# Transposing q of batch 1 with the DMA crossbar instead of TensorE, and the output of half batch 1 in two parts

## Chip, cores and metric

One core of a Trainium2 chip. The time is device microseconds (us) of one execution; a kernel's time is the median of its runs. A run counts as slow when it is over 1.5% above the fastest of its kernel; that happened in gated (one run of four) and early (three of four) alone. "Before" was run beside every other kernel on the same chip; a ratio is the mean time of one kernel's fast runs over that of the other's of the same rounds, with a 95% interval, so it is not quite the ratio of the medians quoted next to it.

## The reference, cut to what matters

Block attention (4 batches, 8 heads, 768 tokens, head size 64), in which keys and values are first mixed by a matrix P that a Sinkhorn iteration makes from `sort_net`; then a feed-forward layer (512 to 2048 to 512) with a squared ReLU.

```python
k_sorted = einsum('bhij,bhjcd->bhicd', P, k_b)      # 8 blocks of 96 tokens
v_sorted = einsum('bhij,bhjcd->bhicd', P, v_b)
attn = softmax(scale * q_b @ k_sb^T)                # within a block
x = (attn @ v_sb)                                   # -> 3072 tokens x 512
out = (s * relu(x @ w_in)**2 + b) @ w_out
```

## The kernel before

TensorE is given the FFN of one half batch while the attention of the next is mixed in between, from a queue of small pieces. Q has to be transposed (`QT`, head size on the partitions). For batches 2 and 3 the DMA crossbar does it (`q_turn`), for batches 0 and 1 TensorE does:

```python
def q_piece(b, hp0, eng):                 # two of the four head pairs
    ...
    for i in range(2):
        for t in range(TQ):               # TQ = 6 groups of 128 tokens
            for e in range(2):
                nc.tensor.transpose(out=ps[e*64:(e+1)*64, i, t*128:(t+1)*128],
                                    in_=qr[b][:, 2*(hp0+i)+e, t, :], identity=ident)
    evac(QT[b][:, hp0:hp0+2, :]..., ps[:, :, 0:S]..., eng)

def q_turn(b):
    for t in range(TQ):
        nc.sync.dma_start(out=QT[b][:, :, t*128:(t+1)*128],
                          in_=qr[b][:, t].rearrange("p h d -> p (h d)"), transpose=True)
```

Mixed V of batch 1 goes through DRAM, because the next step wants another layout: `v_piece1` writes it in 12 pieces ("dv"), `v_read` reads it back in two halves ("vs", 6144 runs of 128 bytes). Both use the sync engine's queue, which issues in program order.

```python
    V1(4)(); V1(5)()                       # last dv writes
    q_piece(1, 0, "s")
    ...
    csums(0, 8)                            # GpSimd: sums of w_out
    v_read(1, nc.sync)
    ffn1(1, ...)                           # FFN of half batch 1, first layer
    load_v(*brows(3))
    csums(8, NF)                           # GpSimd, until about 64.6 us
    qu = Queue([nothing, seq(lambda: q_piece(1, 2, "s"), K(1, 0, 16, "v")), nothing,
                seq(K(1, 32, 16, "s"), K(1, 64, 16, "v")), nothing,
                seq(lambda: load_k(*brows(2)), lambda: load_q(2), bias_piece),
                V2[0], S2(2, 0), V2[1], S2(2, 2), V2[2], V2[3], P2(2, 0), ...], 24)
    ffn2(0, qu)                            # P2(2, 0) is the first product with vs
```

`load_k` of batch 2 (64 rows of 12 KB) and `load_q` of batch 2 (6144 runs of 128 bytes) stand in that queue.

The softmax here doesn't subtract the row's maximum and nothing guards it: scores larger than these inputs give would overflow.

## Time and profile before

| | before |
|---|---|
| time, median of 3 runs | 231.67 us (231.25 to 231.69) |
| span of the profiled run | 229.8 us |
| TensorE busy | 223.2 us, 97% |
| first product with vs starts | 75.62 us |

In the profile's lines PE is TensorE, PEld its loading of weights, DVE VectorE, ACT ScalarE, POOL GpSimd and SPq the sync engine's queue; L342 is line 342 of the kernel. The timeline of the sync queue (start, length, issuing queue, line, what):

```profile
38.59 16.51 SPq L342 DMA_DIRECT2D dv<-vn  x12
62.30 2.27 SPq L361 DMA_DIRECT2D vs<-dv  x2
```

then that of GpSimd:

```profile
64.59 0.54 POOL L97 DMA_DIRECT2D kb<-in_k_dram  x1
65.13 5.29 POOL L84 DMA_DIRECT2D qr<-in_q_dram  x6
```

The vs read is asked for at 62.30, k of batch 2 at 64.59, q of batch 2 from 65.13 on. The read has a head start of 2.3 us.

### The profile page before, as it was taken

How to read it: one execution, taken by the hardware profiler on the slowest of the kernel's cores; microseconds unless marked ns; L12 is line 12 of the kernel's file. 1: busy time of each engine (PE TensorE's matmuls, PEld its weight loads, DVE VectorE, ACT ScalarE, POOL GpSimd, SP SyncE). 2: the span in 40 equal slices, each digit the busy share in tenths (PEclk: the TensorE clock that was granted, in tenths of full speed). 3: DMA queues.
4: the chain of work that ended last, by engine and by line, in shares of the span. 5: the costliest groups of instructions: out<-in, count | busy, mean ns of one | idle time of the engine just before them, and what ended most of it. 6: DMA issues, size and time to landing. Idle time of an engine off the chain costs nothing.

```text
span 229.8 us, 4833 instructions
## 1 busy us (share of the span) xinstructions
PE 223.2 (97%) x2034; PEld 136.3 (59%) x2034; DVE 116.0 (50%) x244; ACT 115.7 (50%) x165; POOL 48.1 (21%) x62
## 2 busy tenths in 40 slices
PE   8979999999999999999999999999999999999994
PEld 5879888765554565665555555655555556654442
DVE  4778666638991554344345843434443634441221
ACT  5268479685358387866621285565322245660000
POOL 7920000299992000008730000000000000000000
PEclk9995699999999999999999999999999999999999
DMA  5899999999399998645999996610115250001212
GB/s 93 137 199 214 223 195 205 227 219 203 70 122 180 314 247 136 126 116 70 133 142 150 183 176 134 76 47 0 49 46 121 87 114 0 3 0 46 86 54 91
DMA packets 46694, 28.90 MB, mean 126 GB/s; under 512 B 35920, under 2 KB 41040, under 8 KB 46160
## 3 DMA queue, kind: packets, MB, share of 16 engines
q0 software_dynamic: 18800, 15.21, 46.5%
q1 hardware_dynamic: 27728, 13.32, 26.8%
q8 instruction: 16, 0.26, 0.5%
q10 hardware_dynamic: 144, 0.07, 0.1%
q14 instruction: 6, 0.05, 0.1%
HBM read 29.63 MB, written 8.65 MB: 167 GB/s over the span
## 4 chain that ended last, share of the span: by engine, by line
PE 80%; DMA 14%; ACT 3%; DVE 1%; issue 0%; SPq 0%
PE hps L498 31%; PE ops L552 30%; DMA dv<-vn 8%; DMA vs<-dv 6%; PE wp L182 6%; PE pv L402 4%; PE sc L375 3%; PE tv L320 2%; PE ops L537 2%; PE tk L294 1%; ACT ks L240 1%; PE tq L254 1%; ACT qt L240 1%; PE tv L350 0%; ACT rt L513 0%
## 5 line engine op out<-in xcount | busy, mean ns | idle before, releaser
L498 PE MATMUL hps<-xt,wi 128*128 128x384 bf16 (+1 forms) x576 | 87.0, 308 | 0.2
L552 PE MATMUL ops<-wo,gt 128*128 128x512 bf16 x368 | 85.8, 379 | 0.0
L498 PEld LDWEIGHTS <-wi 128*128 128x128 bf16 x576 | 53.7, 98 | 30.6 <-issue 1.1
L513 ACT ACTIVATE rt<-hps 128x768 bf16<-128x768 f32 (+1 forms) x72 | 53.1, 740 | 37.0 <-PE hps L498 36.1
L514 DVE TENSOR_TENSOR gt<-rt 128x768 bf16<-128x768 bf16 (+1 forms) x72 | 41.6, 580 | 49.5 <-ACT rt L513 49.3
L552 PEld LDWEIGHTS <-gt 128*128 128x128 bf16 x368 | 34.0, 98 | 37.9 <-issue 0.6
L378 ACT ACTIVATE at<-sc 96x768 bf16<-96x768 f32 x32 | 24.4, 803 | 30.2 <-PE sc L375 30.1
L526 DVE SCALAR_TENSOR_TENSOR ot<-ops,s_bc,bias 128x512 f32<-128x512 f32 x23 | 17.2, 750 | 40.4 <-PE ops L552 40.3
L407 DVE TENSOR_TENSOR x<-pv,rec 96x512 bf16<-96x512 f32 (+1 forms) x36 | 22.6, 628 | 1.3
L240 ACT CAST ks<-tk 64x512 bf16<-64x512 f32 (+1 forms) x32 | 18.6, 582 | 4.2 <-PE tk L294 3.9
L674 POOL TENSOR_TENSOR csum<-csum,wo 128x512 f32<-128x512 f32 x14 | 17.6, 1254 | 1.0
L182 PE MATMUL wp<-zt 128*128 128x256 bf16 x84 | 13.5, 329 | 1.1 <-DVE warm L113 1.1
L402 PEld LDWEIGHTS <-at 96*128 96x128 bf16 (+1 forms) x256 | 12.0, 104 | 4.3 <-DMA vs<-dv 0.8
L238 DVE CAST ks<-tk 64x512 bf16<-64x512 f32 (+1 forms) x20 | 13.1, 654 | 2.1 <-PE tk L294 1.8
L402 PE MATMUL pv<-vs,at 96*128 96x66 bf16 (+1 forms) x256 | 13.0, 199 | 0.4 <-DMA vs<-dv 0.3
L240 ACT CAST vn<-tv 128x512 bf16<-128x512 f32 (+1 forms) x12 | 9.4, 800 | 6.8 <-DMA out_dram<-ot 3.8
L84 POOL DMA_DIRECT2D qr<-in_q_dram x12 | 10.6, 913 | 5.3 <-DMA kb<-in_k_dram 2.9
L375 PEld LDWEIGHTS <-ks 64*96 64x96 bf16 x256 | 8.3, 128 | 5.7 <-issue 4.3
L406 DVE RECIPROCAL rec<-pv 96x8 f32<-96x8 f32 (+1 forms) x36 | 6.9, 193 | 9.1 <-PE pv L402 9.1
L182 PEld LDWEIGHTS <-zt 128*128 128x128 bf16 x84 | 9.5, 117 | 3.2 <-DVE warm L113 1.1
L375 PE MATMUL sc<-qt,ks 64*96 64x96 bf16 x256 | 10.7, 219 | 0.0
L240 ACT COPY qt<-tq 128x768 bf16<-128x768 bf16 (+1 forms) x6 | 5.9, 1014 | 5.0 <-PE tq L254 3.3
(72 smaller groups left out, 97.5 us busy)
## 6 DMA issues: line engine op xcount, KB each, us to landing
out_dram<-ot SPq DMA_DIRECT2D x23, 256.0 KB, 2.8
kb<-in_k_dram POOLq DMA_DIRECT2D x4, 768.0 KB, 11.1
vb<-in_v_dram POOLq DMA_DIRECT2D x4, 768.0 KB, 18.9
wi<-in_moe_w_in_dram POOLq DMA_DIRECT2D x2, 1024.0 KB, 19.6
wo<-in_moe_w_out_dram POOLq DMA_DIRECT2D x2, 1024.0 KB, 32.5
qr<-in_q_dram POOLq DMA_DIRECT2D x12, 128.0 KB, 17.7
dv<-vn SPq DMA_DIRECT2D x6, 256.0 KB, 6.6
vs<-dv POOLq DMA_DIRECT2D x4, 384.0 KB, 13.1
```

Of the source, the lines that this page charges most:

```text
L182: nc.tensor.matmul(out=wp, lhsT=zt[:, 0:128], rhs=zt, start=True, stop=True)
L240: nc.scalar.copy(out=out, in_=in_)
L375: nc.tensor.matmul(out=sc[:, e, n * BLK:(n + 1) * BLK], lhsT=ks[pr, g0 + n, :], rhs=QT[b][pr, hp, q0:q0 + BLK], start=True, stop=True)
L378: nc.scalar.activation(out=at, in_=sc[:, :, 0:TG], func=AF.Exp, scale=scale)
L402: nc.tensor.matmul(out=pv[e][0:m, (n - n0) * VW:(n - n0 + 1) * VW], lhsT=atf[:, c0:c0 + m], rhs=VS[b][:, gi, :], start=True, stop=True)
L407: nc.vector.tensor_tensor(out=x[:, n0:n0 + nn, hp * 128:(hp + 1) * 128].rearrange("p n (e d) -> p e n d", e=2), in0=pvv[:, :, :, 0:D], in1 ...
L498: nc.tensor.matmul(out=hps[:, f, 0:nt], lhsT=wi_at(hp, f0 + f), rhs=xt_at(t, hp, n0, nn), start=(hp == 0), stop=(hp == NHP - 1))
L513: nc.scalar.activation(out=rt[:, :, 0:nt], in_=hps[:, :, 0:nt], func=AF.Relu)
L514: nc.vector.tensor_tensor(out=gt[:, f0:f0 + 2, c0:c0 + nt], in0=rt[:, :, 0:nt], in1=rt[:, :, 0:nt], op=ALU.mult)
L526: nc.vector.scalar_tensor_tensor(out=ot, in0=ops, scalar=s_bc, in1=bias, op0=ALU.mult, op1=ALU.add)
L552: nc.tensor.matmul(out=ops, lhsT=gt[:, f, m * 128:(m + 1) * 128], rhs=wo_at(f), start=(f == 0), stop=(f == NF - 1))
L674: nc.gpsimd.tensor_tensor(out=csum, in0=csum, in1=wo_at(f), op=ALU.add)
```

## The change

The intent: take 48 transposes from TensorE, which works 97% of the time, and let the crossbar do them. The load has to become token-major for that: within a partition the eight heads of one token lie side by side, and the runs shrink from 768 to 128 bytes. Since the first `q_piece` had filled TensorE's wait for the copy of the transposed output, that output is now transposed and copied in two parts.

```diff
     def load_q(b, part=slice(0, 128)):
-        if b > 1:
+        if b > 0:
             qr[b] = qrp.tile([128, TQ, H, D], BF, tag="qr", name=f"qr{b}")
             for t in range(TQ):                    # six loads, 64-element runs
...
-    def q_piece(b, hp0, eng):   (removed)
...
-                   seq(V1(2), V1(3)), lambda: t_piece(1, "v")], 8), 2, 2)
+                   seq(lambda: t_part(1, 0, "s", 0, HB), V1(2), V1(3)),
+                   lambda: t_part(1, 2, "v", 0, HB)], 8), 2, 2)
     V1(4)()
     V1(5)()
-    q_piece(1, 0, "s")
...
     csums(0, 8)
+    q_turn(1)
     v_read(1, nc.sync)
...
-    qu = Queue([nothing, seq(lambda: q_piece(1, 2, "s"), K(1, 0, 16, "v")), nothing,
+    qu = Queue([nothing, K(1, 0, 16, "v"), nothing,
```

## The prediction

> **What bounds the kernel now.** I read the page first (busy shares, then the chain of work that ended last), then the chain in order of time, then the DMA queues stretch by stretch between 34 and 86 us, where everything that the change touches happens. The page:
>
> ```profile
> span 229.8 us, 4833 instructions
> PE 223.2 (97%) x2034; PEld 136.3 (59%) x2034; DVE 116.0 (50%) x244; ACT 115.7 (50%) x165; POOL 48.1 (21%) x62
> ```
>
> TensorE works 97% of the span. Of its 6.6 us without work about 1.1 lie ahead of the first matmul and 3.4 after the last one, so the middle is a nearly unbroken row of matmuls: what shortens TensorE's list shortens the kernel, unless a wait takes its place. The chain in order of time (start, length, what) says where such a wait stands ready:
>
> ```profile
> 42.82 11.82 DMA dv<-vn
> 54.66 7.50 DMA dv<-vn
> ...
> 62.69 12.89 DMA vs<-dv
> 75.62 0.71 PE pv L402 x16
> ```
>
> For 33 us, from 42.8 to 75.6, the chain is not TensorE at all. V of batch 1, mixed by the sort matrix, is written to DRAM in 12 pieces (dv) and read back in another layout (vs), and the first product that needs it starts the moment it lands. The list of TensorE's waits between 37 and 95 us puts the price at only
>
> ```profile
> PE pv L402 <- DMA vs<-dv: 0.3, 1, 0.3
> ```
>
> (total, times, longest). So at 75.6 us two chains meet almost exactly: TensorE's own work, and a DMA round trip with no slack to speak of. The whole change lies ahead of this meeting point.
>
> The tile view of qr gives the transposes that go away (ns min/median/max, starts):
>
> ```profile
> L269 PE MATMUL tq<-ident,qr x48: 218/219/244, 45.8 to 60.1; 128*64 128x128 bf16 x48
> L279 SPq DMA_TRANSPOSE qt<-qr x12: 1197/1216/2528, 91.7 to 147.2; - x12
> ```
>
> and the timeline shows that they don't cost 48 times 219 ns, because they are pipelined:
>
> ```profile
> 45.81 0.86 PE L269 MATMUL tq<-ident,qr 128*64 128x128 bf16 x24
> 59.41 0.86 PE L269 MATMUL tq<-ident,qr 128*64 128x128 bf16 x24
> ```
>
> Last, the load queue of the DMA (q0) in two stretches of 4 us, 34 to 38 and 82 to 86 (packets, MB landed, share of 16 engines):
>
> ```profile
> q0 software_dynamic: 958, 0.81, 127.9%
> ```
>
> ```profile
> q0 software_dynamic: 2708, 0.34, 133.6%
> ```
>
> The first moves runs of 768 and 1024 bytes at about 200 GB/s of bf16. The second is q of batch 2, already loaded token-major, in runs of 64 elements (128 bytes): 677 packets per us, but only 85 GB/s.
>
> **What the Trainium skill says.** "DMA: Bandwidth & Descriptors", section Specifications, gives 512 B as the least transfer for line rate; the two lines above agree in direction (85 against 200 GB/s). The same page, section Queues, rings and completion order, says that each engine takes turns between the queues that have work for it, at packet granularity. The trace agrees: the dv writes issued at 38.6 us, beside short packets, landed in 5.3 us, and those of 43 us, which drained beside the 12 KB rows of k, in 11.8 us. "Advanced Engine Details and Errata", section X-Bar Transpose (TRN2), calls crossbar transposes as fast as regular DMAs. No view isolates one here; what I see is issue on the sync queue, 1.2 us each, 2.5 us to landing. "TensorE: Matmul & The Clock Gate", section Part 4: PE-mode transpose, reports about 275 ns for one in a kernel; 219 ns is recorded here, and 36 ns apart is what 24 of them cost the engine.
>
> **The change, part by part.**
>
> 1. TensorE loses 48 transposes: 2 x 0.86 = 1.72 us. This is the most that the change can take from the engine's list. ScalarE loses two 1.44 us copies of qt, which delayed nothing that TensorE waited for.
>
> 2. The first 0.86 us is a filler. Before, it ran at 45.8 while VectorE copied all of xt for half batch 1 (0.94 us from 45.72), and the FFN started at 46.72, right behind both. Now that copy is split: four transposes' worth of heads on ScalarE (0.80 us for 128x768, as the qt copies of that form take) ahead of two vn copies, the rest on VectorE (0.55 us) after the last gt. I walk it: t_part ends on TensorE at 43.7; ScalarE copies it until 44.6, two vn follow (0.47 apart) until 45.5, the last rt until 46.0; VectorE makes gt until 46.45 and the second xt until 47.0. TensorE, through with V1 at 46.2, does two products on the first half of xt (0.33 us) and waits for the second until 47.0. Work equal to a start at 46.7: the gain of this half is about 0.05 us. The extra copy on ScalarE gives back what the filler cost.
>
> 3. The second 0.86 us (59.4) is real up to the next wait. At 65.17 TensorE multiplies csum, which GpSimd finishes at about 64.75 (14 additions of 1.25 us, last start 63.5). TensorE would now come at 64.3, so about 0.4 us of wait appears and some 0.45 us of gain remains, if the second half of w_out, which the last eight additions read, is there by 54.1 as before (it landed at 12.72 + 36.3 = 49.0).
>
> 4. The load of q grows from 1024 packets of 768 bytes to 6144 of 128. At 200 GB/s the old one is 3.9 us (the trace: from 37.95, w_out's first half, to 41.85). At 677 per us the new one is 9.1 us. Everything behind it in the same queue moves by about 5.3 us: w_out's second half from 49.0 to 54.3, k of batch 1 from 51.8 to 57 (first used about 59.3), the two v loads of batches 2 and 3 from 55.6 and 62.0 to about 61 and 66 (first used about 66.2). Each lands within a microsecond of its need. GpSimd's six issues (0.9 us each instead of one) wait for earlier loads' slots but are ahead of the queue's need.
>
> 5. Six crossbar transposes go onto the sync queue between the last dv write and the vs read: 6 x 1.2 = 7.3 us of issue, plus 0.79 MB of traffic. In the old pace (last dv write issued at 54.7) they would end at 62.4, where the vs read was issued anyway (62.3). If the dv writes come sooner, because they now meet 128-byte packets until 47 instead of 12 KB rows, the transposes start about 48 and the vs read could be issued at 56 to 58.
>
> Sum on TensorE alone: 0.05 + 0.45, and the 0.3 us of the old wait, if vs lands a microsecond earlier: -0.5 to -1.2 us.
>
> **The rivals.**
>
> A. Clean gain: the dv writes land faster, vs is issued before 60, all loads just make it. For it: the DMA was only 30% busy with loads from 58 to 62, so there is air; and small packets overlap with another queue's large ones (in 82 to 86 us q1 moved 0.70 MB beside those 2708). Time 230 to 231.
>
> B. The wait takes its place: the DMA engines carry 5.3 us more of q and an estimated 3 us of transposes before the same deadline, so vs or the last v load comes late. From 47.2: 5.2 for w_out, 3.9 for each of k, v, v, 2 for dv, 3 for transposes, 9.1 for the vs read (6144 packets) make 78 without overlap, against the 74.9 at which TensorE now wants vs; with k of batch 2 in between, up to 82. For it: the same sum for before, 41.85 + 5.2 + 11.7 + 2 + 9.1 + 3.9 = 73.8, is close to the real 75.6. Time 232 to 237.
>
> C. TensorE waits earlier: w_out's second half comes at 55 instead of 54.1, csum slips 1 us, and the product for the bias with it. This eats the gain and leaves 231.5 to 232.5.
>
> D. Nothing: vs lands where it did, and TensorE waits out what it saved: 231.4.
>
> Against a large effect in either direction: the ceiling of 1.72 us, and the fact that after 76 us nothing of the list changes.
>
> **Range and chances.** A gain beyond 2% would need 4.6 us and TensorE gives up 1.7, so its chance is 0.01. A loss beyond 2% needs the full, unoverlapped sum of B: 0.09. I weigh A at 0.45, C and D together at 0.3, B at 0.25, and put the time at 231.1 us, with 229.4 to 235.2 as the range.
>
> **What would show it.** Right for step 1: no line for tq<-ident,qr of form 128*64, TensorE's busy time 221.5. Step 2: a wait of TensorE of about half a microsecond near 46.5 for the xt copy. Step 3: csum as releaser of the bias product. Step 4: w_out's second half landing at 54 to 55, longer loads of k. Step 5: dv writes of 42 to 47 us landing in under 6 us and the vs read issued before 60; if it is issued after 62 or lands after 75, B holds. The prediction is wrong if the token-major load drains much faster or slower than 677 packets per us, if crossbar transposes stall the other traffic while they run, or if the vs wait disappears and more than 1.7 us is won.

## The result, and the profile after

242.45 us (median of 4 runs, 242.25 to 243.07) against 231.46 beside it: ratio 1.0483, interval 1.0455 to 1.0511. The change makes the kernel 4.8% slower. The page of the changed kernel:

```profile
span 240.7 us, 4740 instructions
...
PE 223.3 (93%) x1967; PEld 136.4 (57%) x1986; DVE 118.6 (49%) x244; ACT 113.6 (47%) x164; POOL 52.7 (22%) x67
```

TensorE's busy time has not fallen although it has 48 transposes fewer; we come to that. (Its count has fallen by 67: 19 matmuls of the output layer are missing from this trace.) The chain in order of time:

```profile
60.45 1.33 SPq L265
61.88 1.22 SPq L265
63.19 1.22 SPq L265
64.50 1.22 SPq L265
65.81 0.54 SPq L347
66.40 17.86 DMA vs<-dv
84.39 1.09 PE pv L388 x16
85.49 1.71 PE ops L538 x4
```

L265 are the crossbar transposes. The sync queue works through them and comes to the vs read (L347) at 65.81; the read's second half then needs 17.86 us where it needed 12.89; the product that waits for it starts at 84.39 instead of 75.62. The waits of TensorE (total, times, longest):

```profile
PE pv L388 <- DMA vs<-dv: 8.1, 1, 8.1
PE hps L484 <- DVE xt L238: 1.1, 1, 1.1
```

The timelines of the sync queue, then of GpSimd, answer to those of before:

```profile
39.44 16.79 SPq L328 DMA_DIRECT2D dv<-vn  x11
...
56.33 9.39 SPq L265 DMA_TRANSPOSE qt<-qr  x6
...
65.81 8.61 SPq L347 DMA_DIRECT2D vs<-dv  x2
```

```profile
64.93 0.55 POOL L97 DMA_DIRECT2D kb<-in_k_dram  x1
65.46 5.29 POOL L84 DMA_DIRECT2D qr<-in_q_dram  x6
```

The read is now asked for 0.9 us after k of batch 2, not 2.3 us ahead of it. In the DMA queues between 66 and 70 us (packets, MB, share of 16 engines), before:

```profile
q1 hardware_dynamic: 2436, 0.31, 128.1%
q0 software_dynamic: 21, 0.26, 34.5%
```

and after:

```profile
q0 software_dynamic: 44, 0.54, 92.7%
q1 hardware_dynamic: 328, 0.08, 10.7%
```

Before, q1 (the sync queue) moves 2436 packets of vs in these 4 us. After, it moves 328, none of vs, while q0 moves two thirds of k.

One more loss follows from the wait. This is the stretch after it (window; its length; then busy us and instructions of PE, PEld, DVE, ACT, POOL; granted TensorE clock; DMA share; GB/s):

```profile
84.40:87.00 2.60, 2.60 (x21) 1.48 (x22) 1.69 (x4) 0.00 (x0) 0.00 (x0) 0.50 1.05 405
87.00:90.00 3.00, 3.00 (x19) 1.32 (x18) 0.00 (x0) 1.01 (x1) 0.00 (x0) 0.55 0.23 89
```

TensorE comes back at half its clock. "TensorE: Matmul & The Clock Gate", section Why this matters for your kernels, warns of gaps over about 3 us between bursts; the trace agrees, with 0.50 after a gap of 8.1 us. By these two lines the half clock lasted some 5.3 us after the wait. Slow matmuls count as busy: at half the clock 5.3 us hold about 2.7 us of extra busy time (an estimate), more than the 1.7 us of transposes that went away.

The sum, between landmarks of the two chains. Up to the first product with vs: 84.39 - 75.62 = 8.77 us. From there to the first layer for half batch 2 (102.30 and 90.99 us): 17.91 - 15.37 = 2.54 us, close to the estimate for the clock. From there to the end: 138.40 - 138.81 = -0.41 us. Together 10.9 us, the difference of the spans.

### The profile page after: what moved, and what is told of

Same layout as the page of the kernel before. It is cut to its first block, busy times and chain, and to the rows that moved or that the text cites. A ratio compares the mean times of both kernels' runs of the same rounds, so it can differ in the third digit from the quotient of the medians.

```text
span 240.7 us, 4740 instructions
## 1 busy us (share of the span) xinstructions
PE 223.3 (93%) x1967; PEld 136.4 (57%) x1986; DVE 118.6 (49%) x244; ACT 113.6 (47%) x164; POOL 52.7 (22%) x67
## 4 chain that ended last, share of the span: by engine, by line
PE 73%; DMA 14%; POOL 4%; SPq 3%; ACT 2%; issue 2%; DVE 1%; POOLq 0%
PE hps L484 30%; PE ops L538 29%; DMA vs<-dv 7%; DMA qr<-in_q_dram 4%; PE pv L388 4%; PE sc L361 3%; POOL csum L660 3%; DMA vb<-in_v_dram 3%; SPq L265 2%; PE tv L306 2%; PE ops L523 1%; PE tk L280 1%; ACT ks L240 1%; PE tq L254 1%; PE wp L182 1%
## 5 line engine op out<-in xcount | busy, mean ns | idle before, releaser
L538 PE MATMUL ops<-wo,gt 128*128 128x512 bf16 x349 | 84.7, 385 | 1.6 <-DVE ot L512 0.4
L500 DVE TENSOR_TENSOR gt<-rt 128x768 bf16<-128x768 bf16 (+1 forms) x72 | 44.9, 630 | 48.2 <-ACT rt L499 48.0
L538 PEld LDWEIGHTS <-gt 128*128 128x128 bf16 x368 | 34.5, 99 | 39.1 <-issue 2.6
L388 PE MATMUL pv<-vs,at 96*128 96x66 bf16 (+1 forms) x256 | 13.6, 203 | 8.2 <-DMA vs<-dv 8.1
L84 POOL DMA_DIRECT2D qr<-in_q_dram x18 | 15.9, 901 | 21.3 <-DMA wi<-in_moe_w_in_dram 10.0
L388 PEld LDWEIGHTS <-at 96*128 96x128 bf16 (+1 forms) x256 | 12.6, 107 | 12.5 <-issue 9.1
L660 POOL TENSOR_TENSOR csum<-csum,wo 128x512 f32<-128x512 f32 x14 | 17.6, 1255 | 1.0
L240 ACT CAST vn<-tv 128x512 bf16<-128x512 f32 (+1 forms) x12 | 9.4, 811 | 17.6 <-PE tv L336 17.5
L182 PE MATMUL wp<-zt 128*128 128x256 bf16 x84 | 12.5, 313 | 1.1 <-DVE warm L113 1.1
L361 PE MATMUL sc<-qt,ks 64*96 64x96 bf16 x256 | 10.8, 219 | 0.0
L182 PEld LDWEIGHTS <-zt 128*128 128x128 bf16 x84 | 9.0, 112 | 2.7 <-DVE warm L113 1.1
## 6 DMA issues: line engine op xcount, KB each, us to landing
kb<-in_k_dram POOLq DMA_DIRECT2D x4, 768.0 KB, 10.6
```

The source lines that it names most:

```text
L182: nc.tensor.matmul(out=wp, lhsT=zt[:, 0:128], rhs=zt, start=True, stop=True)
L240: nc.scalar.copy(out=out, in_=in_)
L361: nc.tensor.matmul(out=sc[:, e, n * BLK:(n + 1) * BLK], lhsT=ks[pr, g0 + n, :], rhs=QT[b][pr, hp, q0:q0 + BLK], start=True, stop=True)
L388: nc.tensor.matmul(out=pv[e][0:m, (n - n0) * VW:(n - n0 + 1) * VW], lhsT=atf[:, c0:c0 + m], rhs=VS[b][:, gi, :], start=True, stop=True)
L500: nc.vector.tensor_tensor(out=gt[:, f0:f0 + 2, c0:c0 + nt], in0=rt[:, :, 0:nt], in1=rt[:, :, 0:nt], op=ALU.mult)
L538: nc.tensor.matmul(out=ops, lhsT=gt[:, f, m * 128:(m + 1) * 128], rhs=wo_at(f), start=(f == 0), stop=(f == NF - 1))
```

## The experiments

All outputs were correct. Times are medians; "vs wait" is TensorE's longest wait for the read in the profiled run.

| run | what it is | us | ratio to before | vs wait |
|---|---|---|---|---|
| after | the change | 242.45 | 1.0483 | 8.1 |
| swap | vs read ahead of the transposes | 243.03 | 1.0504 | none (QT: 10.6 in all) |
| late | meant to delay k and q of batch 2 | 242.92 | 1.0510 | 9.3 |
| load_only | before + token-major load | 231.22 | 0.9998 | none |
| split_only | before + split of the output transposes | 231.90 | 1.0039 | none |
| gated | after; k and q of batch 2 after vs | 237.63 | 1.0230, unclear | none (k: 4.2) |
| vsact | after; vs read issued by ScalarE | 242.40 | 1.0483 | 9.4 |
| early | after; transposes after the second dv pair | 255.7 to 272.0 | no verdict | 16.1 |
| tok_wide | load_only + wide TensorE transposes | 232.83 | 1.0073 | none |
| hold | before; vs read held to 65.2 us | 241.31 | 1.0439 | 7.8 |
| gate_q | after; only q of batch 2 after vs | 239.07 | 1.0329 | 5.8 |
| no_split | after without the split | 242.14 | 1.0478 | 10.8 |
| cure | gated on half of vs, k of batch 2 used later | 234.34 | 1.0149 | none |

My first theory (O) was the order on the sync queue: the transposes hold the read back. The rivals were the short packets of the load (L), the split copy (S), and the crossbar traffic itself (X). Sorting the trace's packet records by queue and size gives a second measure, the first and last packet of each transfer (us; 128-byte packets are vs, 12 KB packets k of batch 2):

```
            vs asked for   vs packets        k of batch 2
before         62.30     63.28 to 74.96    68.61 to 73.18
swap           62.22     63.20 to 74.90    69.11 to 73.77
hold           65.18     69.18 to 81.97    65.81 to 71.21
after          65.81     70.64 to 83.42    66.38 to 72.38
gate_q         67.43     73.16 to 80.66    65.91 to 71.91
gated          66.04     67.21 to 75.45    79.12 to 85.09
```

**load_only** and **split_only**: the two smaller parts alone.

```diff
 load_only (against before): token-major load, TensorE transposes kept
-        if b > 1:
+        if b > 0:
-                        in_=qr[b][:, 2 * (hp0 + i) + e, t, :], identity=ident)
+                        in_=qr[b][:, t, 2 * (hp0 + i) + e, :], identity=ident)
 split_only (against before): the t_part lines of the change, nothing else
```

> Kernel before with q of batch 1 loaded token-major and transposed by TensorE as before. Rival L: vs lands several us later than 75.6, time 234 or more. Theory O: second half of w_out lands within 1.5 us of 49.0, vs within 1.5 us of 75.6, time 231.0 to 233.

> Kernel before with only the split of the transposes of half batch 1. Rival S: the FFN of half batch 1 starts over 1 us later than at 46.7 and the time rises by more than 1 us. Theory O: TensorE's list is the same length and the q transposes still fill the gap behind the copy; time within 0.8 us of before, 230.7 to 232.3.

The load costs nothing: 231.22 against 231.08, ratio 0.9998 (0.9978 to 1.0018), and the last vs packet at 74.53 against 74.96. Rival L is out. The split costs 0.4% (interval 1.0005 to 1.0072), at the edge of what I had allowed theory O. Its chain shows how:

```profile
45.64 0.40 ACT rt L513
46.07 1.06 DVE gt L514
47.13 0.48 DVE xt L238
```

The second half of the copy stands behind the last gt on VectorE, and that gt takes 1.06 us here, while GpSimd does its sums, instead of the 0.36 us of the ones ahead of it. So the FFN starts at about 47.6 and not at 46.72. That the sums slow it was not tested.

The time hides one more thing. In split_only the read was asked for at 61.03, 1.3 us earlier than in before, and its last packet came at 69.78, 5.2 us earlier. K of batch 2 began at 68.68, when most of the read was through: with so little company it takes 8.8 us from request to last packet, where it takes 12.7 in before.

**swap**: the read goes first.

```diff
 swap (against after)
-    q_turn(1)
-    v_read(1, nc.sync)
+    v_read(1, nc.sync)
+    q_turn(1)
```

> Changed kernel with the vs read issued ahead of the six crossbar transposes. Theory O (the order on the sync queue holds the vs read back from 62.3 to 65.8 us and so puts it beside k and q of batch 2): read issued near 62.3 to 62.8, landing at 75 to 77, TensorE's wait for vs under 1.5 us, a new wait of 1 to 4 us for QT of batch 1 near 69 us; time 231 to 235. Rival X (the crossbar traffic itself slows the read): read lands at 79 or later, time 236 or more. Rival L (token-major load) and rival S (split copy): time stays within 1.5 us of 242.4, since neither is touched.

The read did what theory O said (last packet at 74.90), and the time did not: 243.03. TensorE now waits for the transposes:

```profile
PE sc L361 <- DMA qt<-qr: 10.6, 3, 8.3
```

Their first packet came at 74.28, though the first was issued at 64.85. They stand behind the read in the same queue, as the read had stood behind them. A theory that names one order only, as O does, falls: in either order the second of the two is late. Rivals L and S, which expected about 242.4, got the time right for a reason that the wait refutes.

**late**: a miss of mine.

```diff
 late (against after)
-                seq(lambda: load_k(*brows(2)), lambda: load_q(2), bias_piece),
+                bias_piece,
...
-                V2[2], V2[3], P2(2, 0),
+                V2[2], V2[3], seq(P2(2, 0), lambda: load_k(*brows(2)), lambda: load_q(2)),
```

> Changed kernel with the loads of k and q of batch 2 issued after the first product that needs vs, instead of before it. If the company of these loads makes the read long: read still issued near 65.8 but lands in 10 to 11 us instead of 17.9, at about 76 to 77; TensorE's wait under 1.5 us; time 232 to 235 (unless k of batch 2 then comes late, which would show as a wait for kb near 85). If the late issue alone or the crossbar counts: landing stays past 80 and time above 238.

GpSimd issued k at 64.57 all the same. A place in the program delays nothing on an engine that waits for nothing, so the run tests nothing; it repeats the result of after (242.92). The next run makes GpSimd wait for data.

**gated**: k and q of batch 2 wait for vs.

```diff
 gated (against after)
+    def vs_gate():
+        for p in (0, 64):                          # one element of each half
+            g = sk.tile([1, 1], BF, name=f"vg{p}")
+            nc.gpsimd.tensor_copy(out=g, in_=VS[1][p:p + 1, 63, D - 1:D])
-                seq(lambda: load_k(*brows(2)), lambda: load_q(2), bias_piece),
+                seq(vs_gate, lambda: load_k(*brows(2)), lambda: load_q(2), bias_piece),
```

> Changed kernel; GpSimd copies one element of each half of the landed vs before it issues k and q of batch 2, so that these two loads cannot run beside the vs read (the run called late did not do this: GpSimd issued them at 64.6 us all the same). Theory C (company: the read lands late because 64 rows of k and 6144 short packets of q share the engines with it): read issued near 65.8, landed by 76 to 78, TensorE's wait for vs 0.3 to 2 us; time 232 to 236, with a small new wait for k of batch 2 possible. Rival X (crossbar traffic or the late issue alone): read lands past 80, time above 238.

The read, asked for as late as in after (66.04), needs 9.34 us by the chain and TensorE does not wait for it. Its list of waits:

```profile
PE tk L280 <- DMA kb<-in_k_dram: 4.2, 1, 4.2
PE hps L484 <- DVE xt L238: 1.1, 1, 1.1
```

So neither the late issue by itself nor the crossbar traffic makes the read long: the company does. The time is 237.63 (234.39 to 239.64, the last of them a slow run). The three fast runs spread so far that the interval of the ratio, 1.0154 to 1.0306, leaves the verdict unclear. The time stays above before because k of batch 2 now comes late. That was foreseen as possible, but it was larger than expected and put the time past the range that theory C, the company, had been given.

**gate_q**: only q waits.

```diff
 gate_q (against after)
-                seq(lambda: load_k(*brows(2)), lambda: load_q(2), bias_piece),
+                seq(lambda: load_k(*brows(2)), vs_gate, lambda: load_q(2), bias_piece),
```

> Changed kernel with only q of batch 2 held until vs has landed; k of batch 2 stays just ahead of the read. If k's 64 long rows do the harm: first vs packets still near 70.6, landing at 79 to 81, wait 3 to 5 us, time 235 to 239. If q's short packets do it: first packets near 67, landing at 76 to 78, time 231.5 to 235. If both are needed for the full loss: in between, but below 240.

239.07, wait 5.8 us: in between, as expected if both are needed, but only just outside the ranges given for k alone (235 to 239, wait 3 to 5), so time and wait hardly decide. The packets say which does what. With k there and q away, the read starts as late as ever (73.16, 1.2 us after the last row of k) but drains in 7.5 us instead of 12.8. K of batch 2 delays the start, q of batch 2 stretches the rest.

**hold**: the test without the change. The kernel before, with head-major load and TensorE transposes; the read waits on the sync queue for a 4-byte store of GpSimd's last sum.

```diff
 hold (against before)
-    v_read(1, nc.sync)
     ffn1(1, Queue([nothing] * 4 + [build_pd2] + [nothing] * 3, 8))
     load_v(*brows(3))
     csums(8, NF)
+    hold = dram.tile([1, 1], FP, name="hold")
+    nc.sync.dma_start(out=hold, in_=csum[0:1, 0:1])
+    v_read(1, nc.sync)
```

> Kernel before, no crossbar transpose of batch 1, head-major load, TensorE transposes; the only edit holds the vs read on the sync queue behind a 4-byte store of csum, so it is issued near 65.3 us, just after k of batch 2 (64.6) instead of 2.3 us ahead of it. Theory F (the two requests change places, and the one that comes second waits and then shares): first packets of vs near 69 to 71 instead of 63.3, landing at 80 to 85, TensorE's wait for vs 5 to 9 us, time 238 to 243. Rival X (the crossbar transposes are what slows the read): read lands at 78 to 79, wait 3 us, time 234 to 235.5.

241.31, ratio 1.0439 (1.0415 to 1.0464): over 90% of the loss (10.2 of 11.0 us), with none of the change's parts. Its sync queue, and TensorE's waits:

```profile
64.66 0.27 SPq L681 DMA_DIRECT2D hold<-csum  x1
65.18 8.18 SPq L361 DMA_DIRECT2D vs<-dv  x2
```

```profile
PE pv L402 <- DMA vs<-dv: 7.8, 1, 7.8
```

The read is asked for 2.9 us later than before and 0.6 us after k of batch 2 (64.57); its first packet moves from 63.28 to 69.18, its last from 74.96 to 81.97. This is theory F, and it holds: the two requests change places, and 2.9 us of delay become 7 us. Rival X expected 234 to 235.5.

**vsact** and **early**: moving the read or the transposes.

```diff
 vsact (against after): v_read(1, nc.sync) removed;
+    qu = Queue([nothing, K(1, 0, 16, "v"), lambda: v_read(1, nc.scalar),
 early (against after): q_turn(1) removed from its place;
+                   ... P(1, 2), seq(V1(1), lambda: q_turn(1)), P(1, 3),
```

> Changed kernel with the vs read issued by ScalarE at about 62 to 63 us, so it waits for no transpose on the sync queue; the transposes stay where they are and run beside it, and so do k and q of batch 2. If the sync queue's order is half of the delay: read lands at 77 to 80, time 233 to 238. If all that counts is the sum of traffic between 56 and 80 us: read lands past 82 and time above 239.

> Changed kernel with the six transposes issued right after the second pair of dv writes, in the stretch (44 to 55 us) in which the sync queue otherwise waits for dv writes to land. Both theories that blame the place (62 to 66 us) of the transposes expect a vs read issued near 62 to 64, landing at 75 to 78, no wait for QT, time 231 to 236. If the crossbar transposes cost the same wherever they stand: dv writes end late, vs lands past 80, time above 239.

vsact did not help: 242.40. The read started early (first packet 64.11) but ran beside the transposes, then beside k and q, and its last packet ended at 85.17. Half of its packets were through at 67.8, 3.6 us after the first, as fast as in gated (67.21 to 71.0); then came hardly one until 71.9, while the rows of k moved, and the rest crawled beside q. It had been asked for at 62.56, ahead of k, so the order of the two requests does not decide alone: the sum of what is in flight matters too. This is what the second branch of the expectation said.

early was the largest miss. Placed among the loads of w_out, k and v, the six transposes did this to the sync queue:

```profile
38.77 4.83 SPq L328 DMA_DIRECT2D dv<-vn  x4
43.64 44.04 SPq L265 DMA_TRANSPOSE qt<-qr  x6
87.77 12.69 SPq L328 DMA_DIRECT2D dv<-vn  x8
```

44 us for six issues, which took 9.39 us in after. And the DMA queues in its stretch from 62 to 66 us:

```profile
q1 hardware_dynamic: 147, 0.04, 108.8%
q0 software_dynamic: 16, 0.15, 28.1%
```

Both queues have work, and both almost stand still: 0.19 MB in 4 us. In after, in the same stretch with no load in flight, q1 moved 2325 packets. So in this trace transposes and 12 KB rows hold each other up. The runs spread from 255.67 to 271.98, and the profiled one counts as slow, so I take no number of the loss from them; even the fastest is 24 us over before.

**no_split**: the change with the old single copy (the two t_part lines turned back).

> Changed kernel with the transposes of half batch 1 in one piece as before. If the loss is in the vs read alone, as theory F has it: read still lands at 83 to 85, time 241 to 244, and what the split gains or costs ahead of it is swallowed by the wait. If the split matters: time differs from 242.5 by more than 1.5 us.

242.14: the same as after, as expected. What happens ahead of the read disappears in the wait for it.

**tok_wide**: a try at a better kernel, on load_only. With token-major q, two heads lie side by side and one transpose can take both.

```diff
 tok_wide (against load_only)
-                for e in range(2):
-                    nc.tensor.transpose(out=ps[e * 64:(e + 1) * 64, i, ...],
-                        in_=qr[b][:, t, 2 * (hp0 + i) + e, :], identity=ident)
+                nc.tensor.transpose(out=ps[:, i, t * 128:(t + 1) * 128],
+                    in_=qr[b][:, t, 2 * (hp0 + i):2 * (hp0 + i) + 2, :]..., identity=ident)
```

> Kernel before with the token-major load, and TensorE transposes two heads at once: 12 matmuls of 128x128 for 24 of 128x64 in each of the two places. If the cost on TensorE is by instruction: 0.43 to 0.55 us instead of 0.86 in each place, time 230.3 to 231.3, 0 to 0.8 us below before. Not slower than load_only (231.2).

A miss. Its timeline of TensorE at the second place, where the kernel before has 24 matmuls in 0.86 us:

```profile
59.26 0.83 PE L268 MATMUL tq<-ident,qr 128*128 128x128 bf16 x12
```

Half as many instructions, twice as wide, take the same time. The median of 232.83 (231.29 to 234.68) is no gain either; the profiled run, the fastest, had a span of 229.6.

**cure**: the whole loss away?

```diff
 cure (against after): as gated, but vs_gate waits for the first half only, and
-                seq(T(2), S2(3, 0), K(2, 0, 16, "s")), P2(3, 0), nothing,
-                seq(S2(3, 2), K(2, 32, 16, "s")), nothing, P2(3, 2),
+                seq(T(2), S2(3, 0)), P2(3, 0), nothing,
+                seq(S2(3, 2), K(2, 0, 16, "s")), nothing, seq(P2(3, 2), K(2, 32, 16, "s")),
```

> Changed kernel; k and q of batch 2 are held until the first half of the vs read has landed (about 74 us), and the products that need k of batch 2 stand three slots later in the queue. Theory F says that this takes away the whole loss: vs issued near 66, lands at 76 to 78, wait under 1.5 us, no wait for k of batch 2 above 1 us, time 230.3 to 233. If something else in the change costs several us, it stays above 234.

234.34, just above the 234 that I had named. The waits for vs and for k are gone, and so is the clock loss; 8.1 of the 11 us are won back. These waits of TensorE are left:

```profile
PE hps L484 <- DMA xt<-x: 1.3, 1, 1.3
...
PE hps L484 <- DVE xt L238: 1.1, 1, 1.1
...
PE tk L280 <- ACT ks L240: 0.8, 1, 0.8
PE tv L306 <- ACT ks L240: 0.4, 1, 0.4
```

The first is another crossbar transpose (x of half batch 2), which landed in 10.98 us with q of batch 2 beside it; in before, also with q beside it, it took 7.6. What made the difference was not tested. Its first product with vs starts at 75.95 by the chain, not earlier than the 75.62 of before: the 1.72 us that TensorE gave up are gone before that point, 1.1 of them in the wait for xt. No version that I ran beats the kernel before.

## Why the prediction was wrong, point by point

**The bound and the meeting point** were read rightly: TensorE's list, and the read of vs with no slack. What I did not read was why the read took 12.89 us and no more. It was ahead of k and q of batch 2 by 2.3 us, and nothing on the page says that this order is chance: it is the difference of two timelines.

**Step 1** is right in count: the tq group of form 128*64 is gone. The busy time I gave as its sign (221.5) was not seen: the lower clock more than makes up for it.

**Step 2** had the mechanism and half the size. TensorE waited 1.13 us, not half a microsecond, and went on at 47.86, not 47.0; the term that was off is the last gt, 1.07 us in place of some 0.4. split_only shows the step as a cost of its own: 1.0039.

**Step 3** (csum as the next wait) was not reached in a way that mattered: the product for the bias started at 65.59 against 65.38.

**Step 4** failed in its size. I took 677 packets per us from a stretch in which that load ran beside large writes of the other queue. Here it drained faster (7.8 us), and above all it overlapped: it ran from 34.96 to 42.74 us, beside w_out's first half, where I had let it begin at 37.95, behind that half. So w_out's second half landed at 33.88 + 16.1 = 50.0, 1.0 us later than before, not 5.3. The k and v loads behind it ended at 61.60 in both kernels. load_only confirms it with the time. With the load, rival C and the bulk of rival B's sum fall.

**Step 5** is the step that failed with consequences. "The dv writes come sooner" was wrong: the short packets were over by 42.7, the writes of 43 us met the same long rows and took 10.8 us. So the transposes began at 56.33, took 9.39 us of the queue where I had 7.3, and the read was issued at 65.81. The 2.1 us more are a wait of the transposes, which the list of the sync queue's waits between 50 and 70 us puts down to the v load with its 12 KB rows:

```profile
SPq L265 <- DMA vb<-in_v_dram: 2.7, 2, 2.2
```

I had compared the time of issue with 62.3 and with 56 to 58, and never with GpSimd's 64.6. The last packet of the read comes 8.5 us later than in before, and the table of packets says where they go. From request to last packet the read takes 8.8 to 9.4 us with little or no company (split_only, gated), 12.7 in before, 13.2 with k alone beside it (gate_q) and 17.6 in after. So k's rows cost it 3 to 4 us on either side of the line; in before they stop it in the middle (110 packets of it from 69 to 72 us). What the crossing adds, as an estimate from these differences, is the 3.5 us of the later request and some 4.4 us of q, which now runs beside the whole read and not beside its end.

**Rival B** named the right wait and far too small a loss. Its sum left out q of batch 2 and the clock after a wait: 84.3 for the landing, where it had 78 to 82, and 2.54 us on top. By the prediction's own list this was to be seen: "if it is issued after 62 or lands after 75, B holds". I gave B a weight of 0.25 and cut the range at 235.2, because I had in mind that the ceiling of the change is 1.72 us. That ceiling bounds the gain, not the loss.

**What stays open.** Why the request that comes second waits some 4 us for its first packet when it is on another queue. In before it was k (asked for at 64.59, first row at 68.61), in hold it was vs (65.18 and 69.18). The runs do not say where it is held. For vs there is an estimate: 64 rows on 16 engines are four each, and a row's packet took 0.93 us (median in before), so an engine that finishes its rows of k first is taken for 3.7 us. The packet records do not name the engine, so this is not shown, and it does not explain why k waits in before. How much of the last microsecond between hold and after belongs to the crossbar and how much to the split was not separated either.

## What to carry to other kernels

Before adding to a queue, list for each later entry which other engine's requests it now stands ahead of, and by how much: a lead of 2 us can be what keeps a transfer short, and 3 us of delay can cost ten. (A lead alone is no guarantee: vsact had it, and the read still ended at 85.17.) To delay a load, make it wait for data; moving its line does nothing on an engine that waits for nothing. Keep crossbar transposes away from loads with long rows, and when TensorE would wait for several microseconds, count the lower clock after it.

## What the Trainium skill lacked or had wrong

- "Advanced Engine Details and Errata", X-Bar Transpose (TRN2): says that transposes are as fast as regular DMAs, and says nothing of what an ordinary load beside them does to their time. Six of them took 9.39 us of issue with the end of one v load in flight, and 44.04 us beside loads with 12 KB rows (run early), with the loads held up as well.
- "DMA: Bandwidth & Descriptors", Queues, rings and completion order: says that an engine drains a whole packet, typically some 9 to 17 descriptors, before it turns to another queue, but not how many rows of 12 KB make a packet or how long a turn can last. In hold the read was asked for at 65.18 and its first packet came at 69.18, when most of the 64 rows of the other queue had started; in before it was the other way round (64.59 and 68.61).
- The same page, Specifications: puts runs under 512 B below line rate, which agrees, but gives no rate for 128-byte runs. It was 85 GB/s in the stretch that the prediction used and 100 GB/s in load_only, where 6144 such packets drained in 7.9 us (34.8 to 42.7) among longer ones. The rate is not a property of the packet size alone.
- "TensorE: Matmul & The Clock Gate", Part 4: gives a time for one transpose, not for a row of them. 24 of 128x64 took 0.86 us, 12 of 128x128 0.83 us.
- The same page, Part 1: the clock comes back after at least one busy window of about 3.4 us; how many it takes the page does not say. Here, after 8.1 us of waiting, it took some 5.3 us (0.50 and 0.55 in the two stretches from 84.4 to 90 us).
